# An unused tile of 464 columns ahead of the right-hand weight tiles of the last stage

## The chip, the cores and the metric

The kernel runs on one core of a Trainium2 chip. The metric is device time in microseconds of one execution; three executions of the kernel before took 3172.34, 3176.55 and 3176.86 us, median 3176.55 us. The trace comes from one further execution, which the profiler recorded.

## The reference, cut to what matters

Three layers follow each other on `x` of 4 x 3072 x 256: a filter in the frequency domain, a gated layer that mixes along the sequence, and a two-layer network with a squared activation. All in float32. The change lies in the stage that computes the second half of the middle layer and the whole of the last:

```
h = relu(x @ w_in);  u, v = halves of h            # 512 columns each
v_s = w_spatial @ normalised(v) + b_spatial        # the long product along the sequence
y = (u * v_s) @ w_out                              # 4 x 3072 x 256
r = relu(y @ w2_in)                                # 256 -> 2048
out = (s * r * r + b) @ w2_out                     # 2048 -> 256
```

## The kernel before, in words

Three stages run one after the other. `attention` computes the filter and `v` up to about 540 us of the span. `mixing` computes the product along the sequence (line 857, moving tiles of 384 columns) up to about 1814 us. `output`, where the change is, computes the rest.

`output` goes over 24 blocks of 512 positions. Each float32 factor is held as two parts, high and low, and each product is made of three passes: high by high, high by low, low by high. A pass is one matmul with a weight block of 128 x 128 and a moving tile of 128 x 512, and every matmul loads its own weight block first. The work of one block on TensorE is 240 such matmuls, always issued in groups of 12 or 24:

- `u_product` (line 1031, two calls): 24 matmuls, weights `w2`, `w3`, moving tile `y_hl`.
- `out_product` (line 1049): 24 matmuls, weights `w4`, `w5`, moving tile `g`.
- `layer1` (line 1068, eight calls, k = 0 to 7): 96 matmuls, moving tile `x_hl`. Calls k = 0 and 1 use `w6` and `w7`, 2 and 3 `w8` and `w9`, 4 and 5 `w10` and `w11`, 6 and 7 `w12` and `w13`. Within a call six matmuls make the first output chunk and six the second; of each six, three are with the even-numbered weight tile and then three with the odd one.
- `layer2` (line 1089, eight calls): 96 matmuls, weights `w14` to `w21`, one tile a call, moving tile `q_hl`.

A loop over steps writes the order out by hand: `layer1` of step j, then at some steps a part of the next block's `u_product` or `out_product`, then `layer2` of step j - 2. ScalarE and VectorE turn `ps_h` of `layer1` into `q_hl` (relu, square, high part, low part: lines 1072 to 1075) and do the same kind of work for the other products. The weights are loaded once, at the stage's start: `w2` to `w12` on SyncE's queue, `w13` to `w21` on GpSimd's (line 965). They are read again in all 24 blocks.

**Where the tiles lie.** Pools of the side "left" are stacked from the low end of each partition of on-chip memory, pools of the side "right" from the high end. In the program as built, the left stack of this stage begins at byte 16,512. All its moving tiles (`x_hl`, `q_hl`, `y_hl`, `g`) and `w6` to `w12` begin at a multiple of 2048 plus 128: `x_hl` at 16,512 and 24,704, `q_hl` at 41,088, 49,280 and 57,472, `w6` at 65,664. The right stack begins with `ones` (8 bytes, in a place of 32) at 229,312; below it come `w21` at 225,216 down to `w13` at 192,448, and `w5` at 188,352 down to `w2` at 176,064. All of these begin at a multiple of 2048 plus 1984. A moving operand is 2048 bytes of each partition and starts at a multiple of 2048 from its tile's start; a weight block is 512 bytes and starts at a multiple of 512 from its tile's start. The highest tile of the left stack, `g`, ends at 170,112.

In `mixing` both operands come from the left stack, `a_hl` at 16,512, 22,656 and 28,800 and `b_hl` at 34,944, 39,040 and 43,136, all at a multiple of 2048 plus 128, with weight blocks at multiples of 512 from there and moving operands at multiples of 512 too. `mixing` also fills the places that the right stack of `output` takes later: `kept` (lines 874 to 878) from byte 192,480 to 229,344, the staging tiles of `convert_half` from 176,256 to 191,616, and the last tile of `a11` from 173,184 to 176,256. A later tile in the same place waits for the earlier one's last reader.

Of the kernel before, what the change touches and what calls it, by code (L numbers as in the profile page):

```python
# [9 lines left out]
F32 = mybir.dt.float32  # L10
# [935 lines left out]
def output(tc, nc, yd, md, chunks, cd, bs, s_in, b_in, out):  # L946
# [6 lines left out]
    mpool = left("o_m", 5)  # L953
    work = left("o_work", 2)
    lines = right("o_line", 1)
    wts_late = right("o_wl", 1)
    wts = right("o_w", 1)
    rot = left("o_rot", 2, space=PSUM)
# [212 lines left out]
def network(ctx, tc, ins, out):  # L1171
# [25 lines left out]
    with tc.manual_schedule():  # L1197
        attention(tc, nc, ins['x'], ins['w_r'], ins['w_i'], ins['b_r'], ins['b_i'],
                  ins['c_f'], ins['c_b'], ins['c_g'], ins['c_v'], ins['c_s'], zd, vd, yd, vn, chunks, cd,
                  lambda: mixing(tc, nc, ins['moe_w_spatial'], vn, md, sd, convert_half)).run()  # L1200
        output(tc, nc, yd, md, chunks, cd, ins['moe_b_spatial'], ins['moe2_s'], ins['moe2_b'], out)
# [25 lines left out]
```

## Time and profile before

| | us |
|---|---|
| median of three runs | 3176.55 |
| the profiled execution's own time | 3178.15 |
| its span, first to last instruction | 3176.4 |
| TensorE busy in the span | 3067.5 (97%) |
| VectorE, ScalarE, GpSimd busy | 2281.9, 1396.0, 392.3 |
| `output` on TensorE, first to last matmul | 1813.6 to 3170.8 |

A matmul's end is modelled in the trace, and one starts before the last has drained; so the busy share of TensorE does not tell how densely it works. The spacing of the starts does, and the chain of waits shows it: where it runs through TensorE alone, the length of a piece divided by the number of matmuls in it is the spacing.

### The profile page before, as it was taken

What the parts mean: (1) busy time and instruction counts of PE and PEld (TensorE: products, weight loads), DVE (VectorE), ACT (ScalarE), POOL (GpSimd) and SP (SyncE); (2) the same over time, 40 slices, a digit from 0 to 9 for tenths busy, and PEclk for the clock granted to TensorE, in tenths of its full rate; (3) what the DMA queues carried; (4) which work ended last, traced back from release to release, by engine and by line L of the source; (5) the groups of instructions that cost most, each with busy time, mean ns of one, the idle gap of its engine ahead of it and who ended that gap; (6) DMA issues with size and microseconds to landing.
All of it is one profiled execution on the core that took longest, in us unless ns stands there. A gap on an engine that the chain in (4) does not pass through costs nothing.

```text
span 3176.4 us, 42089 instructions
## 1 busy us (share of the span) xinstructions
PE 3067.5 (97%) x16040; PEld 2744.1 (86%) x16040; DVE 2281.9 (72%) x3275; ACT 1396.0 (44%) x2068; POOL 392.3 (12%) x497
## 2 busy tenths in 40 slices
PE   6999997999999899999999999999999999999999
PEld 5888986999999899999999868888888888888887
DVE  5888998788878788888878756565565656665564
ACT  5677766433344343433444333343333334343343
POOL 2665534021001200000000100000000000000000
PEclk8999999999999999999999999999999999999999
DMA  8987767596546957465561522111111212112010
GB/s 250 291 274 239 243 213 281 195 339 236 183 160 232 378 185 249 138 233 210 171 220 60 218 94 73 57 57 47 67 50 44 83 33 88 42 38 92 30 37 14
DMA packets 217602, 488.02 MB, mean 154 GB/s; under 512 B 21748, under 2 KB 66616, under 8 KB 217400
## 3 DMA queue, kind: packets, MB, share of 16 engines
q1 hardware_dynamic: 184328, 353.51, 33.3%
q0 software_dynamic: 33072, 131.82, 11.3%
q8 instruction: 126, 2.06, 0.3%
q14 instruction: 76, 0.62, 0.1%
HBM read 322.72 MB, written 162.53 MB: 153 GB/s over the span
## 4 chain that ended last, share of the span: by engine, by line
PE 76%; DVE 13%; DMA 5%; issue 3%; ACT 2%; POOL 0%; SPq 0%; ACTq 0%; DVEq 0%; POOLq 0%
PE acc L857 28%; PE oacc L1089 17%; PE ps_h L1068 16%; PE ps_o L1049 4%; PE ps_u L1031 4%; PE ps_m L414 3%; PE ps_vp L579 2%; DVE kept L874 1%; DVE a_hl L838 1%; DVE b_hl L838 1%; DMA st_b<-vn 1%; PE ps_z L340 1%; PE ps_g L367 1%; DMA st_a<-in_moe_w_spatial_dram 1%; DVE bn L592 1%
## 5 line engine op out<-in xcount | busy, mean ns | idle before, releaser
L857 PE MATMUL acc<-a_hl,b_hl 128*128 128x384 f32 x7056 | 1239.0, 336 | 33.6 <-DVE kept L874 12.1
L857 PEld LDWEIGHTS acc<-a_hl,b_hl 128*128 128x128 f32 x7056 | 1233.4, 189 | 39.2 <-ACT kept L878 13.8
L1089 PE MATMUL oacc<-q_hl,w 128*128 128x512 f32 x2304 | 568.5, 395 | 0.4 <-DVE q_hl L1075 0.4
L1068 PE MATMUL ps_h<-x_hl,w 128*128 128x512 f32 x2304 | 560.7, 392 | 1.9 <-ACT x_hl L1052 1.2
L1089 PEld LDWEIGHTS oacc<-q_hl,w 128*128 128x128 f32 x2304 | 433.0, 188 | 103.8 <-DVE q_hl L1075 0.8
L1068 PEld LDWEIGHTS ps_h<-x_hl,w 128*128 128x128 f32 x2304 | 432.6, 188 | 101.1 <-ACT x_hl L1052 1.6
L834 ACT CAST a_hl<-a 128x768 fp32r<-128x768 f32 x253 | 211.6, 836 | 521.6 <-PE acc L857 442.8
L1073 DVE TENSOR_TENSOR r<-r 128x1024 f32<-128x1024 f32 x192 | 235.1, 1224 | 241.6 <-ACT r L1072 241.6
L1075 DVE TENSOR_TENSOR q_hl<-r,q_hl 128x1024 fp32r<-128x1024 f32 x192 | 235.3, 1225 | 214.5 <-ACT q_hl L1074 214.5
L1072 ACT ACTIVATE r<-ps_h 128x1024 f32<-128x1024 f32 x192 | 197.3, 1027 | 362.9 <-PE ps_h L1068 362.7
L838 DVE TENSOR_TENSOR a_hl<-a,a_hl 128x768 fp32r<-128x768 f32 x253 | 241.3, 954 | 137.3 <-ACT a_hl L834 136.7
L1074 ACT CAST q_hl<-r 128x1024 fp32r<-128x1024 f32 x192 | 201.8, 1051 | 274.9 <-DVE r L1073 274.9
L838 DVE TENSOR_TENSOR b_hl<-b,b_hl 128x512 fp32r<-128x512 f32 x295 | 201.9, 684 | 0.0
L834 ACT CAST b_hl<-b 128x512 fp32r<-128x512 f32 x295 | 181.7, 616 | 0.0
L875 POOL DMA_DIRECT2D md<-kept x112 | 60.4, 540 | 829.6 <-DVE kept L874 825.2
L579 PE MATMUL ps_vp<-win,y_hl 128*128 128x512 f32 x576 | 149.9, 396 | 1.6 <-ACT y_hl L479 1.2
L1031 PE MATMUL ps_u<-y_hl,w 128*128 128x512 f32 x576 | 142.4, 396 | 2.0 <-DVE y_hl L1017 2.0
L1049 PE MATMUL ps_o<-g,w 128*128 128x512 f32 x576 | 139.3, 396 | 3.9 <-ACT g L1038 2.2
L1049 PEld LDWEIGHTS ps_o<-g,w 128*128 128x128 f32 x576 | 108.1, 188 | 31.2 <-ACT g L1038 3.0
L1031 PEld LDWEIGHTS ps_u<-y_hl,w 128*128 128x128 f32 x576 | 108.1, 188 | 28.1 <-DVE y_hl L1017 2.3
L874 DVE TENSOR_TENSOR kept<-acc,kept 128x768 f32<-128x768 f32 x112 | 102.9, 951 | 22.0 <-PE acc L857 21.1
L579 PEld LDWEIGHTS ps_vp<-win,y_hl 128*128 128x128 f32 x576 | 101.2, 189 | 20.2 <-ACT y_hl L479 1.6
(139 smaller groups left out, 3664.0 us busy)
## 6 DMA issues: line engine op xcount, KB each, us to landing
a<-in_moe_w_spatial_dram SPq DMA_DIRECT2D x144, 384.0 KB, 5.1
b<-vn SPq DMA_DIRECT2D x168, 256.0 KB, 5.3
md<-kept POOLq DMA_DIRECT2D x112, 384.0 KB, 5.0
m<-md SPq DMA_DIRECT2D x42, 1024.0 KB, 7.3
st_a<-in_moe_w_spatial_dram SPq DMA_DIRECT2D x72, 384.0 KB, 6.7
vn<-vr POOLq DMA_DIRECT2D x96, 256.0 KB, 4.4
s<-a POOLq DMA_DIRECT2D x48, 384.0 KB, 5.9
x_f<-in_x_dram SPq DMA_DIRECT2D x32, 384.0 KB, 6.6
```

The lines of the kernel that those rows point to most:

```text
L579: nc.tensor.matmul(ps, y[:, a, k, o:o + 128], win[k][:, w, :], start=c == 0, stop=c == 5)
L834: nc.scalar.copy(s[:, 0, :], t)
L838: sub(s[:, 1, :], term.pop((kind, n)), f(s)[:, 0, :])
L857: nc.tensor.matmul(acc[d][:, h, 0:TH], b[:, m, d * 128:(d + 1) * 128], a[:, w, h * TH:(h + 1) * TH], start=fresh and i == 0 and c == 0, st ...
L1031: nc.tensor.matmul(ps[:, d, 0:TB], win[k][:, a, o:o + 128], y[:, w, k, :], start=c == 0, stop=c == 5)
L1049: nc.tensor.matmul(ps[:, h, 0:TB], wo[k // 2][:, a, o:o + 128], g[:, w, k, :], start=c == 0, stop=c == 11)
L1068: nc.tensor.matmul(ps[:, e, 0:TB], w[:, a, o:o + 128], x[:, i, j, :], start=c == 0, stop=c == 5)
L1072: nc.scalar.activation(r, ps, AF.Relu)
L1073: nc.vector.tensor_mul(r, r, r)
L1074: nc.scalar.copy(s[:, 0], r)
L1075: nc.vector.tensor_sub(s[:, 1], r, f(s)[:, 0])
L1089: nc.tensor.matmul(ps[:, h, 0:TB], w[:, a, o:o + 128], s[:, i, e, :], start=ff == 0 and c == 0, stop=ff == 2 * NP - 1 and c == 2)
```

## The change

One tile is allocated in the pool `lines`, ahead of the weight tiles. Nothing writes or reads it. It takes 464 x 4 = 1856 bytes of each partition at the high end, so that everything allocated in `wts_late` and `wts` (`w2` to `w5`, `w13` to `w21`, and the small `s_t`, `b_t`, `cs`) lies 1856 bytes lower. No instruction is added, removed or moved in the order of any engine.

```diff
@@ -953,6 +953,7 @@
     mpool = left("o_m", 5)
     work = left("o_work", 2)
     lines = right("o_line", 1)
+    gap = lines.tile([128, 464], F32, name="gap")
     wts_late = right("o_wl", 1)
     wts = right("o_w", 1)
     rot = left("o_rot", 2, space=PSUM)
```

## Rows read from the trace of the kernel before

**Rows 1.** Busy time by stretch: stretch, length, five engines, granted clock, DMA share.
```profile
0.00:540.00 540.00, 482.88 (x3195) 425.77 (x3196) 447.52 (x999) 369.92 (x793) 272.06 (x274) 0.97 0.81 260
...
1800.00:1880.00 80.00, 67.57 (x297) 52.33 (x296) 46.67 (x42) 20.97 (x22) 6.93 (x13) 0.98 0.54 197
...
2000.00:3000.00 1000.00, 1000.00 (x4314) 810.37 (x4314) 591.45 (x496) 396.06 (x396) 0.00 (x0) 1.00 0.17 58
```

**Rows 2.** Waits from 1880 us on: who for whom, total us, times, longest.
```profile
ACT r L1072 <- PE ps_h L1068: 358.6, 181, 4.6
...
PE ps_o L1049 <- ACT r L1072: 0.2, 1, 0.2
```

**Rows 3.** Chain of waits, one block: start us, length us, what, pieces merged.
```profile
2105.00 5.60 PE ps_o L1049 x24
2110.60 2.80 PE oacc L1089 x12
2113.40 2.79 PE ps_h L1068 x12
...
2118.98 2.75 PE ps_h L1068 x12
...
2143.92 2.80 PE ps_u L1031 x12
...
2157.86 2.79 PE ps_h L1068 x12
2160.65 1.40 PE ps_o L1049 x6
```

**Rows 4.** Chain, half calls of `layer1`: `w6`/`w7` first, second half; `w12`/`w13` likewise.
```profile
2118.98 1.39 PE ps_h L1068 x6
...
2120.37 1.36 PE ps_h L1068 x6
...
2157.86 1.39 PE ps_h L1068 x6
...
2159.26 1.40 PE ps_h L1068 x6
```

**Rows 5.** Chain in `mixing`, inside one product (384 columns).
```profile
1600.00 10.93 PE acc L857 x63
```

**Rows 6.** Chain from the stage's first blocks to its end.
```profile
1865.07 1.14 DVE m L1001
1866.20 1.15 DVE m L1034
1867.35 0.04 issue
1867.39 5.18 PE ps_row L1104 x16
...
1882.14 5.87 PE ps_o L1049 x24
...
3106.76 5.60 PE ps_o L1049 x24
...
3162.40 8.41 PE oacc L1089 x36
3170.81 0.03 issue
```

**Rows 7.** Timeline of the SyncE and GpSimd queues at the stage's start.
```profile
1768.81 0.52 SPq L162 DMA_DIRECT2D cd<-c_w  x1
...
1771.55 0.92 SPq L965 DMA_DIRECT2D w<-cd  x2
...
1815.09 0.54 POOL L875 DMA_DIRECT2D md<-kept  x1 [0.50 <-DVE ones L1125]
1820.66 0.54 POOL L965 DMA_DIRECT2D w<-cd  x1 [5.03 <-DMA m<-md]
```

**Rows 8.** Timeline of TensorE and VectorE there, with idle time before.
```profile
1813.64 0.40 PE L1031 MATMUL ps_u<-y_hl,w 128*128 128x512 f32 x1
...
1842.44 2.96 PE L1089 MATMUL oacc<-q_hl,w 128*128 128x512 f32 x12
...
1861.51 1.22 DVE L1073 TENSOR_TENSOR r<-r 128x1024 f32<-128x1024 f32 x1
1863.84 1.23 DVE L1075 TENSOR_TENSOR q_hl<-r,q_hl 128x1024 fp32r<-128x1024 f32 x1 [1.11 <-ACT q_hl L1074]
```

## The prediction

> **What bounds the kernel now.** I read the busy time by stretch first. From 2000 to 3000 us TensorE is busy for all of the 1000 us with 4314 matmuls, at a granted clock of 1.00, while VectorE is busy for 591 us, ScalarE for 396 and the DMA engines for 17% [rows 1]. The table of waits says the same from the other side: after 1880 us TensorE waits for another engine 0.2 us in all, and the others wait for it [rows 2]. So the last stage is TensorE's, and what counts is the spacing of its matmuls: 1000 / 4314 = 231.8 ns for 512 columns. At the clock's upper level of 2.4 GHz, 512 columns are 213.3 ns; the rest, 18.5 ns, is paid 5760 times.
>
> The chain of waits shows that this rest is not the same everywhere. Through one block, groups of 12 matmuls of `oacc`, `ps_u` and `ps_o` (two in 5.60) take 2.80 us, but most groups of `ps_h` take 2.75 [rows 3]. Per matmul that is 233.3 against 229.2 ns, for instructions of one shape. The groups of 2.80 have weights from the right stack, those of 2.75 from the left. Line 1068 itself holds the control: its calls with `w12` and `w13`, the second of them on the right, take 2.79, with the same moving tile, the same PSUM tiles and the same code [rows 3].
>
> The halves of a call tell more. With `w6` and `w7` the first six matmuls take 1.39 us and the last six 1.36; with `w12` and `w13` the halves take 1.39 and 1.40 [rows 4]. So the first half after a right-hand group is still slow, the second is faster, and where right-hand weights come in between it never gets faster. The spacing depends on what came just before: left-hand weights settle at 1.36 / 6 = 226.7 ns, 13.3 above the columns' own time; a right-hand group stays at 20.0 above it and upsets the next few.
>
> What differs between the sides is the place. A left weight block starts at the same remainder by 512 bytes as the moving operand (128), a right one at another (1984 is 448 above a multiple of 512). `mixing` is the second control: there all operands have remainder 128 by 512, and 63 matmuls of 384 columns take 10.93 us [rows 5], 173.5 each, 13.5 above the 160 ns of their columns. It is the settled excess again, over weight blocks at all four multiples of 512 and across several pairs of tiles, so changing tiles does not by itself bring the slow spacing back.
>
> **The change part by part.** *The move.* 1984 - 1856 = 128, so all right-hand weights get the remainder of the moving tiles. `w2` then begins at 174,208, above the left stack's end at 170,112, so nothing else moves.
>
> *The steady blocks.* A block now takes 5.60 + 8 x 2.80 + 2 x 2.80 + 6 x 2.75 + 2 x 2.79 = 55.68 us by its groups; from 2105.00 to 2160.65 it is 55.65 [rows 3]. If all 20 groups of 12 settle, each takes 2 x 1.36 = 2.72, the block 54.40, 1.25 less. From 1882.14 to 3106.76 there are 22 such blocks [rows 6]: (1224.62 / 22 - 54.40) x 22 = 27.8 us.
>
> *The end.* From 3106.76 to 3170.81 there is the last block's part without a successor, with 23 groups (2 + 9 of `ps_h` + 12 of `oacc`, the last three merged as 36) [rows 6]. 64.05 - 23 x 2.72 = 1.5 us. The evacuation after the last matmul is the same.
>
> *The start.* Before 1867 us TensorE waits for VectorE: `ps_row` is released by line 1034, which stands behind lines 1073, 1075 and 1001 [rows 6, 8] on an engine that hardly pauses. What TensorE saves before that is waited for there; I take 0. Its bounds: if all of it counted, some 190 matmuls by 5 ns, 1.0 us; nothing in these rows makes it a loss. Between 1867 and 1882, three groups settle: 0.2 us.
>
> *The price of the new places.* The edit adds no instruction; it can only change which earlier tile a weight load waits for. `w2` and `w3` are issued at 1771.55, some 2.7 us behind the last store out of the staging tiles, and first read at 1813.64 [rows 7, 8]. Whatever part of a staging tile they now wait for, they have 42 us. `w13` to `w21` are issued in one row from 1820.66, after the last store of `kept` at 1815.09 [rows 7]; `w13` now also lies on a staging tile that was done by 1770, and the last `kept` tiles are waited for as before. The first `layer2` reads `w14` at 1842.44 [rows 8], 22 us after the first load. Cost 0; if the cover were gone, the whole distance from store to load, 5 us, would be the most.
>
> *What is late next.* With steps 2.3% shorter, VectorE goes from 59% to 60.5% and ScalarE from 40% to 41% [rows 1]; neither ends a wait of TensorE now. `q_hl` is read four groups (11 us) after its `ps_h` is done, and four operations of 1.0 to 1.2 us make it. Nothing comes up behind TensorE.
>
> *A rule against it.* The Trainium skill, "SBUF — State Buffer", section "Who interferes with whom", gives TensorE two independent read ports, one for the moving operand and one for the weights, and says that TensorE never waits on anyone. By that the place of a weight tile would be indifferent and the gain zero. The control within line 1068 (2.75 against 2.79) speaks against it, unless the second read port differs by side and not by remainder; the time by the rule is that of the second rival below.
>
> *Sum.* 27.8 + 1.5 + 0.2 = 29.5; I take off 0.5 for groups that settle anew after the stalls near 1880: 29.0. On the profiled execution 3178.15 - 29.0 = 3149.2. That execution is 1.6 above the median of the runs shown, so 3147.6 by the median; I forecast 3148.
>
> Both ends of the unknown spacing of a right-hand group: not below 2.72, since no row of 512 columns is faster; not above 2.80, what it takes now, unless equal remainders hurt across the two stacks, which the left groups and `mixing` (same remainder, the fastest rows) make unlikely. I take 2.72, because `mixing` keeps it through tile changes.
>
> **The rivals.**
> *Half.* Each handover between weights far apart (left to right and back, 16 times a block) upsets the spacing, as the first half after a right-hand group does now. Then all groups are like today's `ps_h` with left weights, 2.75: block 55.00, 0.66 less, in all 22 x 0.66 + 64.05 - 23 x 2.75 = 15.3 us: 3161. For it: in the last stage no row shows a settled state that lasts longer than a half call. Against it: the slow half follows a group with the other remainder, and that goes away.
> *Nothing.* It is the side or the distance between the stacks that counts, not the remainder: no row pairs a left moving tile with a right weight tile at equal remainder. Then groups stay at 2.80: 3176.5.
> *Slower.* TensorE works more densely (213.3 / 226.7 = 94% of its columns' time against 92%), and the granted clock falls in the last stage. Price: a group takes 2.72 / clock; from a clock of 0.977 (54.40 / 55.65) on the gain is gone, and at 0.97, the lowest mean of a long stretch here [rows 1], a block takes 56.08, 0.43 more, by about 23 blocks: 3186. For it: nothing but that the denser state is not shown for long. Against it: the clock is 1.00 over the 1000 us where TensorE never pauses, and below that only in stretches with pauses [rows 1].
>
> **How the numbers follow.** All settle 0.70 (own range 3143 to 3152, the runs' spread of 4.5 us to each side); half 0.17; nothing 0.09; slower 0.04. From 3142 to 3163 holds the first two, 0.87 before mis-sizing, some 0.8 after it. What a measurement can tell from no change is 0.2%, 6.4 us: faster 0.87, same 0.09, slower 0.04.
>
> **What would show it.** In the chain of waits after the change: groups of `oacc`, `ps_u`, `ps_o` of 12 at 2.72 and of `ps_h` at 2.72 too, `w12`/`w13` included, and a block of 54.4 us. `ps_h` at 2.75 and `oacc` at 2.75 would be the half case; `oacc` at 2.80 and `ps_h` at 2.75 that only the side counts. A granted clock under 0.98 from 2000 to 3000 us would be the slower case. A wait of TensorE for a load of `w` before 1870 us would show my price of the places wrong, and waits for VectorE in the steady blocks that something was close behind TensorE.

## The result, and the profile after

The changed kernel takes 3146.95 us (median of four runs, 3145.45 to 3147.91) against 3176.70 us before (four runs, 3172.34 to 3177.41): ratio 0.9909, 95% interval 0.9892 to 0.9926. It is faster by 29.75 us; 29 were forecast. The profiled execution took 3147.44 us with a span of 3145.6.

The busy time by stretch of the changed kernel (stretch, length, TensorE, its weight loads, VectorE, ScalarE, GpSimd, granted clock, DMA share, GB/s) compares with [rows 1]:

```profile
0.00:540.00 540.00, 483.12 (x3195) 426.02 (x3196) 444.73 (x999) 369.62 (x793) 272.50 (x274) 0.97 0.81 260
1800.00:1880.00 80.00, 68.69 (x298) 53.09 (x296) 46.67 (x42) 21.27 (x23) 6.95 (x13) 0.96 0.55 197
...
2000.00:3000.00 1000.00, 1000.00 (x4413) 828.33 (x4412) 605.61 (x508) 406.92 (x407) 0.00 (x0) 1.00 0.17 59
```

The third line shows the gain: in the same 1000 us TensorE works on 4413 matmuls instead of 4314, at the same clock of 1.00. Its busy share is 100% in both and tells nothing. The spacing is 226.6 ns instead of 231.8.

The chain of waits through a block of the changed kernel compares with [rows 3] (start us, length us, what, number merged; line numbers of this stage are one higher than before):

```profile
2098.32 5.44 PE ps_o L1050 x24
2103.76 2.72 PE oacc L1090 x12
2106.48 2.72 PE ps_h L1069 x12
...
2136.40 2.72 PE ps_u L1032 x12
2139.12 2.72 PE oacc L1090 x12
2141.84 2.72 PE ps_h L1069 x12
```

Every group of 12 takes 2.72 us, with weights from the right as with weights from the left, and the fast halves of `ps_h` have become whole calls.

The chain of the changed kernel from the stage's first blocks to its end compares with [rows 6]:

```profile
1864.47 1.15 DVE m L1035
1865.62 0.04 issue
1865.66 5.39 PE ps_row L1105 x16
1871.05 2.76 PE ps_u L1032 x12
1873.81 2.72 PE oacc L1090 x12
1876.53 2.73 PE ps_h L1069 x12
...
1880.42 5.73 PE ps_o L1050 x24
...
3077.51 5.44 PE ps_o L1050 x24
...
3131.91 8.17 PE oacc L1090 x36
3140.09 0.02 issue
```

From the first `ps_o` to the one 22 blocks later it is 1197.09 us instead of 1224.62: 27.5 saved. From there to the end 62.58 instead of 64.05: 1.5. From `ps_row` to the first `ps_o` 14.76 instead of 14.75: nothing. `ps_row` itself is released 1.7 us earlier, 1865.66 against 1867.39. That part is not the change's. The timeline of TensorE at the start of the stage (start, length, engine, line, what) has its first matmul at 1811.91 instead of 1813.64 [rows 8], 1.7 us earlier already:

```profile
1811.91 0.40 PE L1032 MATMUL ps_u<-y_hl,w 128*128 128x512 f32 x1
```

In the experiments below that leave the earlier stages alone, this matmul comes anywhere from 1809.3 to 1813.9 us. So the change itself saved 27.5 + 1.5 = 29.0 us in this pair of traces, and 1.7 are scatter of stages that it doesn't touch.

### The profile page after: what moved, and what is told of

It is laid out like the page before. It is cut to its first block, busy times and chain, and to the rows that moved or that the text cites. A ratio compares the mean times of both kernels' runs of the same rounds, so it can differ in the third digit from the quotient of the medians.

```text
span 3145.6 us, 42088 instructions
## 1 busy us (share of the span) xinstructions
PE 3040.7 (97%) x16040; PEld 2745.0 (87%) x16040; DVE 2279.3 (72%) x3275; ACT 1395.4 (44%) x2068; POOL 393.2 (13%) x497
## 4 chain that ended last, share of the span: by engine, by line
PE 75%; DVE 14%; DMA 6%; ACT 2%; issue 2%; SPq 0%; POOL 0%; ACTq 0%; DVEq 0%
PE acc L857 28%; PE oacc L1090 16%; PE ps_h L1069 16%; PE ps_o L1050 4%; PE ps_u L1032 4%; PE ps_m L414 2%; PE ps_vp L579 2%; DMA st_a<-in_moe_w_spatial_dram 1%; DVE a_hl L838 1%; DVE kept L874 1%; DMA st_b<-vn 1%; DVE b_hl L838 1%; DMA st_b<-t 1%; DMA vd<-v_sb 1%; PE ps_g L367 1%
## 5 line engine op out<-in xcount | busy, mean ns | idle before, releaser
L1069 PE MATMUL ps_h<-x_hl,w 128*128 128x512 f32 x2304 | 553.5, 389 | 1.9 <-ACT x_hl L1053 1.2
L1090 PE MATMUL oacc<-q_hl,w 128*128 128x512 f32 x2304 | 553.4, 389 | 0.5 <-DVE q_hl L1076 0.5
```

What stands on the lines that cost most here:

```text
L1069: nc.tensor.matmul(ps[:, e, 0:TB], w[:, a, o:o + 128], x[:, i, j, :], start=c == 0, stop=c == 5)
L1090: nc.tensor.matmul(ps[:, h, 0:TB], w[:, a, o:o + 128], s[:, i, e, :], start=ff == 0 and c == 0, stop=ff == 2 * NP - 1 and c == 2)
```

## The experiments

The theory was that the spacing depends on how far the start of a weight block lies from the start of the moving operand, by 512 bytes (that is, by the remainder after division by 512); the chief rival, that the right side's place alone cost something. A group whose weights start at the favourable difference is called aligned below. In each kernel here all moving tiles of the stage lie, by the addresses of the built program, at one remainder, and gaps of unused tiles move the weights (in E1 the moving tiles too). The difference is always "weights minus moving operand", and edits are shown against the changed kernel. Only the last experiment was executed several times. The others were executed once, under the profiler, beside the kernel before on the same chip (3177.6 us for the first four, 3179.6 for the next four, 3179.5 for the three after); they are judged by the spacing in their traces, since the stages ahead alone scatter by some microseconds.

### Does the difference count, or the place itself?

**E1** moves moving tiles and weights together, by 192 bytes:

```diff
     late = left("o_late", 2)
+    gap_late = late.tile([128, 48], F32, name="gap_late", bufs=1)
...
-    gap = lines.tile([128, 464], F32, name="gap")
+    gap = lines.tile([128, 416], F32, name="gap")
```

> All tiles of the last stage's moving operands and all its weight tiles lie 192 bytes further on than in the changed kernel, so that both have remainder 320 by 512 instead of 128. Theory (only the difference of the two remainders counts): every group of 12 stays at 2.72 us, 226.67 ns a matmul, about 3147 us. Rival (the weights must lie at certain remainders of their own, 128 among them): groups go to 2.75 to 2.80 us, 3160 to 3180 us.

Measured: 3150.45 us. The chain has the same lengths throughout:

```profile
2101.33 5.44 PE ps_o L1051 x24
2106.77 2.72 PE oacc L1091 x12
2109.49 2.72 PE ps_h L1070 x12
```

At this second place the groups are as short as at the first, so it is not the place by itself that counts. That the difference does is shown by the experiments that follow.

**E2** leaves the right side aligned and puts the left-hand weights off by the 320 bytes by which the right-hand ones were off before:

```diff
     wts_mid = left("o_wm", 1)
+    gap_mid = wts_mid.tile([128, 80], F32, name="gap_mid")
     outs = left("o_out", 1)
+    gap_out = outs.tile([128, 48], F32, name="gap_out")
```

> The right-hand weights stay aligned as in the changed kernel; the left-hand ones, w6 to w12, are moved 320 bytes on, so that they differ from the moving tiles as the right-hand ones did before. Theory (difference of remainders, whichever side): the ps_h groups with w6 to w11 go from 2.72 to 2.80 us and upset the groups behind them, which come to about 2.75; a block takes some 55.3 us, the run 3147 + 23 x 0.9, about 3167 us. Rival (it was the right side's place alone that cost): ps_h stays at 2.72 and the run at 3147 us.

Measured: 3166.62 us. The picture of before is turned round; the chain:

```profile
2108.22 2.72 PE oacc L1092 x12
...
2119.24 2.75 PE oacc L1092 x12
2121.99 2.80 PE ps_h L1071 x12
...
2141.43 2.75 PE ps_u L1034 x12
2144.18 2.72 PE oacc L1092 x12
2146.90 2.80 PE ps_h L1071 x12
```

Now `ps_h`, with left-hand weights, has 2.80, and the group behind it 2.75, as `ps_h` had behind the right-hand groups before; a second aligned group in a row has 2.72. So the side is no cause, and the group behind an unaligned one loses 0.03 us.

### What period does the difference have?

**E3 to E10** put all weights, left and right, at one difference X from all moving tiles. For X = 64 the edit is:

```diff
     wts_mid = left("o_wm", 1)
+    gap_mid = wts_mid.tile([128, 16], F32, name="gap_mid")
     outs = left("o_out", 1)
+    gap_out = outs.tile([128, 112], F32, name="gap_out")
...
-    gap = lines.tile([128, 464], F32, name="gap")
+    gap = lines.tile([128, 448], F32, name="gap")
```

For another X the three tiles have X / 4, (512 - X) / 4 and (1856 - X) / 4 columns.

> All weight tiles, left and right, begin 256 bytes past the remainder of the moving tiles. Theory (equality by 512): no settled state, groups at 2.80 us (233.3 ns) as the right-hand ones before, block 56.0 us, about 3185 us. Rival (a shorter period, 256 or a divisor of it, is enough): all groups at 2.72 us, 3147 us. Other values, below 2.72 too, would say that each difference has a price of its own.

> All weight tiles begin 64 bytes past the remainder of the moving tiles. Theory (equality by 512): groups at 2.80 us, about 3185 us. Rival (a period of 64 or less): 2.72 us, 3147 us. Other values, below 2.72 too, would say that each difference has a price of its own.

Two chains tell these apart, first X = 256, then X = 64:

```profile
2101.69 5.44 PE ps_o L1052 x24
2107.13 2.72 PE oacc L1092 x12
2109.85 2.72 PE ps_h L1071 x12
```

```profile
2106.22 5.60 PE ps_o L1052 x24
2111.82 2.80 PE oacc L1092 x12
2114.62 2.80 PE ps_h L1071 x12
```

Measured: 3150.78 us at 256, 3185.96 at 64. The theory's "by 512" fell: 256 is as good as 0. And 64 gives groups as long as 320 did before the change; 320 is 64 by 256. From these values I made a law: one cycle per 4 bytes, repeating after 64 cycles.

> All weight tiles begin 192 bytes past the remainder of the moving tiles. Theory now (the spacing of 512-column matmuls is 512 plus an excess of cycles at 2.4 GHz that grows by one cycle per 4 bytes of difference and repeats every 256 bytes = 64 cycles: 32 at 0 and 256, 48 at 64 and 320): 80 - 64 = 16 cycles, 220.0 ns, groups of 2.64 us, a block of 52.8 us, about 3147 - 37 = 3110 us. Rival (the price depends on the distance either way, equal or not): as at 64 bytes, 2.80 us, about 3185 us.

> All weight tiles begin 128 bytes past the remainder of the moving tiles. Theory (one cycle per 4 bytes, period 64 cycles): the excess is 64 cycles, 240.0 ns, groups of 2.88 us, about 3147 + 73 = 3220 us, or, if a wait of 64 is the same as none, 0 cycles, 213.3 ns, 2.56 us, about 3075 us. Rival (symmetric distance): the slowest of all, above 2.80 us.

> All weight tiles begin 160 bytes past the remainder of the moving tiles. Theory (one cycle per 4 bytes, period 64 cycles): 72 - 64 = 8 cycles, 216.7 ns, groups of 2.60 us, about 3093 us, or, if some cycles are needed in any case, 72 cycles, 243.3 ns, 2.92 us, about 3240 us. Rival (symmetric distance): between the values of 128 and 192 bytes.

> All weight tiles begin 32 bytes past the remainder of the moving tiles. Theory (one cycle per 4 bytes): 40 cycles, 230.0 ns, groups of 2.76 us, a block of 55.2 us, about 3165 us. Rival (steps of 64 bytes, within which the place doesn't count): 2.72 us and 3147 us, or 2.80 us and 3185 us.

Measured: 3161.77, 3183.19, 3183.34 and 3188.04 us. The law fell in all four. At 192 bytes the groups were at 2.75, neither 2.64 nor 2.80; the chain there:

```profile
2102.46 5.49 PE ps_o L1052 x24
2107.96 2.75 PE oacc L1092 x12
2110.70 2.75 PE ps_h L1071 x12
```

At 128, 160 and 32 they were at 2.80. The last two places were to show whether any beats equality:

> All weight tiles begin 224 bytes past the remainder of the moving tiles (32 short of the next multiple of 256). Seen so far: 226.67 ns at 0 and 256, 228.89 at 192, 233.33 at 32, 64, 128, 160 and 320. Theory now (two settled spacings, 544 and 560 cycles, and only differences close below a multiple of 256 come near the shorter one): between 226.67 and 228.89, groups of 2.72 to 2.75 us, 3147 to 3162 us. Rival (only equality by 256 gives the shorter one, 192 is an accident): 233.33 ns, 2.80 us, about 3185 us. Below 226.67 would be a place better than the changed kernel's.

> All weight tiles begin 96 bytes past the remainder of the moving tiles, the last multiple of 32 by 256 not seen. Theory (everything from 32 to 160 settles at 560 cycles): 233.33 ns, 2.80 us, about 3185 us. Rival (a price for each place): any other value; below 226.67 ns would be a place better than the changed kernel's.

Measured: 3186.59 and 3191.16 us. At 224 the rival was right, 2.80. At 96 the groups have 2.81, more than at any other place, so the theory missed there too, by 1 ns a matmul; its chain:

```profile
2107.06 5.62 PE ps_o L1052 x24
2112.68 2.81 PE oacc L1092 x12
2115.49 2.81 PE ps_h L1071 x12
```

All together, from the count of matmuls between 2000 and 3000 us, at a clock of 1.00 each time. The spacing is 1,000,000 / count in ns; as matmuls cut by the window's ends count too, it comes out about 0.1 ns low. The cycles are at 2.4 GHz: aligned matmuls of 512 columns take 53 ns more than those of 384 [rows 5], which is one such cycle for each of the 128 columns. The last column is the profiled execution's time:

| X by 256 | matmuls in 1000 us | ns | cycles over 512 | us |
|---|---|---|---|---|
| 0 (changed kernel) | 4413 | 226.6 | 32 | 3147.4 |
| 0 (X = 256) | 4413 | 226.6 | 32 | 3150.8 |
| 32 | 4288 | 233.2 | 48 | 3188.0 |
| 64 | 4288 | 233.2 | 48 | 3186.0 |
| 96 | 4270 | 234.2 | 50 | 3191.2 |
| 128 | 4288 | 233.2 | 48 | 3183.2 |
| 160 | 4287 | 233.3 | 48 | 3183.3 |
| 192 | 4370 | 228.8 | 37 | 3161.8 |
| 224 | 4288 | 233.2 | 48 | 3186.6 |

It is not a price per byte: six of the seven unequal places give 48 cycles or a little more on the mean, whatever their distance. The starts of single matmuls in these traces show what a mean hides. At 0 and 256 they follow each other evenly every 226.7 ns, at 64 evenly every 233.3. At 32 and 128 long and short spacings take turns (235 and 231 to 232 ns; 237 to 238 and 229 to 230), at 160 and 192 they repeat in threes (231, 231, 238; 226, 229, 232), and at 96 no short pattern is seen. The right-hand groups of the kernel before, at 320, alternate between 230 to 231 and 236, so 64 and 320 agree in the mean but not in the pattern. Equality by 256 bytes is the best of the eight places, and no place beat the changed kernel.

### Is it the same in another stage?

**E11** puts the weights of the mixing stage, which were aligned all along, off by 64 bytes:

```diff
         t = term[kind, n]
+        if kind == "b" and n == 0:
+            ring.tile([128, 16], F32, tag="gap_b", name="gap_b", bufs=1)
         s = hl[kind, n] = ring.tile([128, 2, t.shape[1]], F32R, tag=kind + "_hl", name=kind + "_hl", bufs=3)
```

> The changed kernel with a gap of 64 bytes in the stage before: there the weight tiles b_hl now begin 64 bytes past the remainder of the moving tiles a_hl; the last stage is as in the changed kernel. Theory (the same mechanism in any dense row of matmuls): the excess over the 160 ns of 384 columns goes from 13.3 to 20.0 ns, 180.0 ns a matmul, in the chain some 63 matmuls in 11.3 us instead of 10.9; 7056 x 6.67 ns = 47 us longer, about 3190 us. Rival (it needs 512 columns, or is proper to the last stage): 173.3 ns and about 3147 us.

Measured: 3154.44 us, some 7 more than the changed kernel and far from 47. Neither expectation was right. From the start of the last matmul of `attention` to that of the first `ps_u` it is 1278.8 us. In all the other traces, whose kernels leave this stretch alone, it is 1267.9 to 1274.8, so 4 us are clear of scatter. The chain has two kinds of stretches in this stage of one and the same kernel:

```profile
949.96 28.09 PE acc L859 x159
...
1347.90 24.27 PE acc L859 x140
```

28.09 / 159 is 176.7 ns, 16.7 over the 160 of 384 columns; 24.27 / 140 is 173.4 ns, the aligned spacing of [rows 5]. With the same operands at the same difference, the row of matmuls sits in one of at least two spacings for hundreds of microseconds. So here a wrong difference only allows a slower spacing, and the loss is smaller than with 512 columns, 3.3 ns against 6.7 where it occurs. What makes the row change from one to the other is not shown.

### One part alone

**E12** aligns only `w13` to `w21` and leaves `w2` to `w5` at their difference of before:

```diff
     wts_late = right("o_wl", 1)
+    gap_early = wts_late.tile([128, 48], F32, name="gap_early")
```

> One part alone: w13 to w21 stay aligned as in the changed kernel, w2 to w5 lie 192 bytes lower, 320 past the moving tiles' remainder by 512, as before the change. Theory (a price for each unaligned group, and about 0.03 us more for the one group behind it, until the spacing has settled again): a block of 5.59 (ps_o) + 2 x 2.79 (ps_u) + 3 x 2.75 (the groups behind) + 13 x 2.72 = 54.8 us against 54.4, 9 us in all, 3156 us, 0.993 of the kernel before. Rival (a handover between unaligned and aligned weights leaves the spacing upset for good): the other groups at 2.75 us too, block 55.2, about 3166 us.

Measured: 3158.84 us (four runs, 3152.53 to 3159.88), ratio 0.9937 to the kernel before, interval 0.9920 to 0.9954. The chain:

```profile
2102.52 5.60 PE ps_o L1051 x24
2108.12 2.75 PE oacc L1091 x12
2110.86 2.72 PE ps_h L1070 x12
2113.59 2.72 PE oacc L1091 x12
...
2140.78 2.80 PE ps_u L1033 x12
2143.58 2.75 PE oacc L1091 x12
2146.33 2.72 PE ps_h L1070 x12
2149.05 2.80 PE ps_u L1033 x12
2151.85 2.75 PE oacc L1091 x12
```

5.60 + 2 x 2.80 + 3 x 2.75 + 13 x 2.72 = 54.8 us a block, as expected. An unaligned group costs 0.08 us and the first group behind it 0.03; the second has recovered. The chain through the two halves of that first group (the `oacc` at 2108.12) shows where it does so:

```profile
2108.12 1.39 PE oacc L1091 x6
...
2109.50 1.36 PE oacc L1091 x6
```

The first six matmuls are slow, the last six are at the settled spacing.

## Why the prediction was right, and where its reasons were not

*The steady blocks* were the forecast's main term, 27.8 us, and brought 27.5. The step that carried it was to read 1.36 us per six from the second half of a `ps_h` call and to hold that this spacing would last. It does: 2.72 for every group. E12 shows why the first halves were slower before: the group behind an unaligned one needs about six matmuls to settle. The missing 0.3 us lie in the first `ps_o` at 1880.42, which took 5.73 instead of the settled 5.44.

*The end* brought 1.5 of 1.5. *The start*: 0 for what comes ahead of `ps_row` was right, since VectorE still releases it. (The bound of 1.0 us there counted some 190 matmuls; the trace has 168 between 1813.64 and 1867.39, by 5 ns 0.8 us. Nothing hung on it.) The three groups behind `ps_row` brought their 0.2 us, 8.21 instead of 8.40, but `ps_row` itself took 5.39 instead of 5.18 and ate it. TensorE stands idle for some 4.5 us ahead of `ps_row`, and the granted clock falls to 0.50, the lower level of 1.2 GHz (1867 to 1870 us before the change). The first matmuls of `ps_row` then start at spacings of up to 427 ns: seven of them before the change, eight after, where the rest take about 232. One more at the lower level is the 0.2 us. How many there are varies from run to run, and `ps_row` takes 5.24 to 6.59 us in E1 to E12.

*The 0.5 taken off* for groups that settle anew rested on no row. It came out as the 0.3 of the first `ps_o` and the 0.2 of `ps_row`; that the sum of 29.0 was met to a tenth is in that part luck.

*The price of the new places* was 0, as forecast. No wait for a weight load is in the chain at the stage's start, and what releases `ps_row` is the same row of VectorE's operations. *What is late next*: nothing; VectorE went to 61% and ScalarE to 41%, as worked out.

*The rivals.* "Half" is refuted by the chain. "Nothing" is refuted by the time and by E2. E3 and E4 differ in the place of the weights alone, and by 35 us. The Trainium skill, "SBUF — State Buffer", section "Who interferes with whom", gives TensorE independent read ports for the two operands; as far as that would make the place indifferent, these runs disagree with it. Whether the two reads wait for each other at a port is not shown by that; only that their places together set the spacing. "Slower" is refuted: the clock was 1.00 from 2000 to 3000 us with TensorE working more densely.

*Wrong in the reasons.* The difference counts by 256 bytes, not by 512 (E3); the forecast was right because both give the same answer here. And `mixing` was a weaker control than I took it for: its excess of 13.5 ns looked like proof of alignment, but with 384 columns a difference of 64 bytes keeps the same spacing for long stretches (E11). The control that held was the one with the same shape, line 1068 with `w6` to `w11` against `w12` and `w13`.

*Open.* Why the spacings are what they are. The runs show that the difference of starts sets their mean, that differences equal by 256 bytes have the same mean in the two pairs tried (0 and 256, 64 and 320), that they settle, and that an unaligned group upsets the next. That the weight load's reads and the moving operand's get into each other's way would fit, but no run took one of the two away. Differences that are not a multiple of 32 bytes were not tried, nor other shapes than 384 and 512 columns with weights of 128 x 128. `ps_row`, whose weights have two columns, gives no support: before the change its weights and moving tiles began at equal remainders, and its last matmuls started every 229 to 234 ns. There are too few of them to tell.

## What to carry to other kernels

Where TensorE never waits, judge it by the spacing of its matmuls (matmuls counted in a stretch without pauses), group by group, and not by its busy share. If groups of one shape differ, compare the start addresses of their weights and moving operands; with 512 columns of float32, equal remainders by 256 bytes gave the shortest spacing seen and cost one unused tile. Pools that grow from opposite ends of the memory can get different remainders by themselves, as they did here (128 and 1984 by 2048).

## What the runs showed of the hardware that was not expected

A dense row of matmuls with 512 columns, each with its own weight load, settles at 544 cycles each (226.67 ns) where weights and moving operand start at equal remainders by 256 bytes. At six of the seven unequal places tried it takes 560 cycles or a little more on the mean, at 192 bytes 549; of all these places only 64 gives even spacings. With 384 columns at 64 bytes' difference both 173.4 and 176.7 ns occur in one run. After an unaligned group the next needs about six matmuls before it is back at its own spacing.
